# Nine passes of the sequence DFT as seven block products instead of eight, with two weight chunks prepared elsewhere

## The chip, the cores and the metric

The kernel runs on one core of a Trainium2 chip. The metric is the time of one execution in microseconds (us); the median of three runs stands for a kernel. Five engines run in order, each its own queue, and wait for one another by semaphores: TensorE (PE; PEld are its weight loads), VectorE (DVE), ScalarE (ACT), GpSimd (POOL) and SyncE (SP), which issues the transfers.

## The reference

One FNet block and one gated feed-forward, each behind a layer norm, on x of 2048 x 448:

```
a  = einsum("bsd,ed->bse", ln(x), dft_hid_re)
b  = einsum("bsd,ed->bse", ln(x), dft_hid_im)
h  = x + einsum("ts,bse->bte", dft_seq_re, a) - einsum("ts,bse->bte", dft_seq_im, b)
h2 = h + einsum("bsf,fd->bsd", gelu(ln(h) @ w_gate) * (ln(h) @ w_up), w_down)   # f = 1792
```

The DFT matrices are inputs, 2048 x 2048 and 448 x 448.

## The kernel before, in words

**Numbers in two halves.** Every float32 operand is split into a high and a low float16 half: `hi_part` (line 108, ScalarE) makes the high one, `lo_part` (lines 112 and 114, VectorE) the low one from the source and the high one. A product is then three matmuls, high by high, high by low, low by high.

**The sequence DFT** comes first: 64 steps (`N_STEPS`). Steps 0 to 15 accumulate rows 0 and 1 of the blocks; from step 16 on, four steps make a pass, that is half of one row pair `p`, from 2 to 7. A unit of weights, `ws`, belongs to each step: loaded by SP into `wr`, split by ScalarE and VectorE some steps ahead. A pass in the plain form is 4 x 24 matmuls `acc` of 128 x 448 (line 644). From step `FAST` = 32 on, a pass is done as seven block products (Strassen's scheme) instead of eight: 4 x 42 matmuls `acc_f` of 128 x 224 (line 521). For that, VectorE adds blocks of the unit (`fast_sums`, lines 471 to 473, tile `sums`), ScalarE and VectorE split the raw blocks and the sums (tiles `ws..._0` and `ws..._1`), and the combined operands T of the normed input, eight pairs of blocks, are made once by GpSimd (`t_sums`, tile `tx`) and split (`t_hi`, `t_lo`, tiles `t`). The accumulated banks are combined by `fast_out` (tile `e`) into `zs`.

**The hidden DFT** of each of the eight row pairs follows inside the sequence DFT. The rows are transposed (`z_turn`, line 669) and multiplied with `wh` in two groups, `y_p_0` and `y_p_1`: 21 matmuls of 448 columns each (line 730). Both groups of a pair use one bank of PSUM in turn. The residual is put into the bank first, by ScalarE (`hid_seed`, line 711), and the matmuls add to it; then ScalarE reads it three times (`hid_out`, lines 719 to 721). So the second group's matmuls wait for ScalarE's seed, which waits for its three reads of the first.

**Weights of the feed-forward** come in 14 chunks, `f`. `Weights` loads a chunk (`gu_raw`), makes sums (`gu_s`, lines 328 to 331, VectorE) and splits raw and sums (`gu_w`), and `store` writes it to memory for later units. Eight chunks are prepared beside the sequence DFT (`DFT_F`), the six others beside the feed-forward's units (`JIT_F`), where unit t uses chunk t at first. The feed-forward's first 14 units (lines 1044 and on) take 39 matmuls of 512 columns each; the hidden DFT of the last pair stands in the second of them.

**The order** is written out by hand. Two tables, `early` and `after`, say what is recorded ahead of a step's matmuls and what after its first or second half; each engine's queue has its instructions in the order in which they are recorded. The order within a step is: loads, split of plain units, `fast_sums` with its splits, `early`, matmuls with `after`:

```
    fast_at = [FAST + n for n in (-4, -2, -1)] + list(range(FAST + 1, N_STEPS - 2))
    ...
        if n in fast_at:
            unit = fast_at.index(n) + FAST
            fast_sums(unit)
            ...
            if n < FAST or n % 4 < 3:
                fast_raw(unit)
                fast_split(unit)
    ...
        at(early, m - 2, lambda p=p: hid_seed(p, 0))
        for g in range(2):
            place = last if g else (m, 0)
            at(after, place, lambda p=p, g=g: hid_mm(p, g), lambda p=p, g=g: hid_out(p, g))
            if g == 0:
                at(after, (m, 0), lambda p=p: hid_seed(p, 1))
```

For pair 1, `m` is 24 and `last` is (25, 0): `y_1_0` stands in the middle of step 24, `y_1_1` in the middle of step 25. For pair 2 they stand in steps 29 and 31.

**PSUM.** `ps_seq` gives its seven banks out in turn to `acc` and `acc_f`; when the DFT is over, `ps_ff` takes the same seven banks for the feed-forward, in the order of its names.

Of the kernel before, what the change touches and what calls it, by code (L numbers as in the profile page):

```python
# [32 lines left out]
def kernel(  # L33
# [39 lines left out]
    nc = tc.nc  # L73
# [31 lines left out]
    w_dram = [dram.tile([P, 28 * P], F16, name=f"w_dram{f}") for f in range(NF)]  # L105
# [65 lines left out]
    def w_tile(name, k):  # L171
        return ring.tile([P, 28 * P], F16, tag=f"w{k}", bufs=1, name=name)
# [126 lines left out]
    def ffn_transpose(q, j, parts):  # L299
        xs = ffn[q, j][2]  # L300
        ops = hops[q if q > 1 else 0]
        c = (2 * q + j if q < 2 else j) * P
        for n in parts:
            s0, s1 = ((0, 8), (8, 16), (16, 22), (22, 25))[n]
            nc.sync.dma_start_transpose(ops[:, s0:s1, c : c + P], xs[:, s0 * P : s1 * P])
# [110 lines left out]
    N_STEPS = NT + 8 * (NP - 2)  # L416
# [32 lines left out]

    FAST = N_STEPS - 32
    A_RAW = ("A12", "A11", "A22")
    FORMS = ("S3", "S1", "S2", "S4")
    T_OPS = ("T1", "T3", "T4", "T2")
# [289 lines left out]


    gu, gw = {}, {}
    DFT_F = ((13, 14, 0), (11, 16, 1), (9, 18, 0), (7, 20, 1), (5, 22, 0), (3, 24, 1), (1, 27, 0), (0, 30, 0))
    JIT_F = range(2, 13, 2)

    early, after = {}, {}

    def at(where, n, *what):
        where.setdefault(n, []).extend(what)
# [2 lines left out]
        at(early, 5 + 2 * n, lambda n=n: wh_load(n))  # L757
        at(early, 7 + 2 * n, lambda n=n: wh_split(n))

    def gw_first(f):  # L760
        gw[f] = w_tile(f"gw{f}", f)
        nc.sync.dma_start(gw[f], w_dram[f])

    for i, (f, n, k) in enumerate(DFT_F):
        ahead = 4 if i < 2 or n - DFT_F[i - 2][1] > 4 else 3
        at(after, (n - ahead, 0), lambda f=f, k=k: gu.update({f: Weights(f, k)}))
        at(early, n, lambda f=f: gu[f].sums())
        if f == 0:
            at(early, n + 2, lambda: gu[0].split(True))
            at(early, n + 3, lambda: gu[0].split(False), lambda: gw.update({0: gu[0].w}))  # L770
            at(after, (n + 5, 0), lambda: gu[0].store())
            continue
        at(early, n + 1, lambda f=f: gu[f].split(True))
        at(early, n + 2, lambda f=f: gu[f].split(False))
        at(after, (n + 3, 0), lambda f=f: gu[f].store())


    at(after, (N_STEPS - 3, 1), lambda: gw_first(1))

    turns = [(16, 0), (20, 1), (25, 1), (32, 0), (40, 0), (48, 0), (57, 0)]  # L780
    for p, (n, half) in enumerate(turns):
        b, j = divmod(p, 2)
# [14 lines left out]
        if b < 2:  # L797
# [4 lines left out]
            at(early, n2, lambda b=b, j=j: ffn_split(b, j))  # L802
            for k in range(4):
                at(after, (n2 + 1 + k // 2, k % 2), lambda b=b, j=j, k=k: ffn_transpose(b, j, (k,)))
    at(after, (N_STEPS - 5, 0), lambda: gu.update({JIT_F[1]: Weights(JIT_F[1], JIT_F[1] % 3)}))
    at(after, (N_STEPS - 6, 0), lambda: gu.update({JIT_F[0]: Weights(JIT_F[0], JIT_F[0] % 3)}))
    at(early, N_STEPS - 1, gelu_table)
    at(after, (N_STEPS - 2, 0), lambda: down_load(0), lambda: down_load(1))
    for j, n in ((6, 14), (7, 16), (0, 18), (1, 20), (4, 22), (5, 24), (2, 28), (3, 30)):
        at(early, n, lambda j=j: t_sums(j))  # L810
        at(after, (n, 1), lambda j=j: t_hi(j))
        at(after, (n + 1, 0), lambda j=j: t_lo(j))

# [470 lines left out]
    for q, t0, step, when in ((2, 5, 3, AT_A), (3, 14, 6, AT_B)):  # L1284
# [22 lines left out]
    right.close()  # L1307
    ps_ff = {
        tag: ctx.enter_context(tc.tile_pool(name=f"ps_{tag}", bufs=1, space=bass.MemoryType.PSUM, reuse_waits="tile"))
        for tag in ("a0", "a1", "a2", "a3", "Z", "Y", "X")  # L1310
    }
    ps_ff["tr"] = ps_tr

# [11 lines left out]
    for t in range(NF):  # L1325
        w = gu.get(t + 2) if t + 2 in JIT_F else None
        n = PREP_AT.get(t)
# [70 lines left out]
        do(t, 3)  # L1398
        if w:
            w.store()  # L1400
        if w and w.f + 4 in JIT_F:
            gu[w.f + 4] = Weights(w.f + 4, (w.f + 4) % 3)
        if n is not None and 2 <= n + 2 < NC:
            down_load(n + 2)
        do(t, 4)
# [10 lines left out]
    for t in range(NF, N_GU):  # L1416
# [169 lines left out]
```

## Time and profile before

| what | value |
|---|---|
| median of 3 runs (lowest, highest) | 699.07 us (698.65, 700.11) |
| the profiled execution | 699.87 us, of which its span 698.1 us |
| granted TensorE clock | 1.00 |
| busy shares: TensorE, VectorE, ScalarE, GpSimd | 99%, 82%, 56%, 24% |
| sequence DFT with seven hidden pairs | 6.2 to 336.9 us |
| steps 24 and 25 on TensorE | about 123.6 to 140.6 us |
| feed-forward | 336.9 to 698.1 us |

The span is from the first to the last instruction of the profiled execution; its time contains 1.8 us besides. In rows of a timeline the first number is the start from the span's beginning, the second the time taken, both in us; in brackets stands idle time ahead and what ended it. A row of groups ends with busy us, mean ns of one, and idle time ahead. Matmuls overlap, so a group's mean is longer than the distance from one to the next.

### The profile page before, as it was taken

What the parts mean: (1) busy time and instruction counts of PE and PEld (TensorE: products, weight loads), DVE (VectorE), ACT (ScalarE), POOL (GpSimd) and SP (SyncE); (2) the same over time, 40 slices, a digit from 0 to 9 for tenths busy, and PEclk for the clock granted to TensorE, in tenths of its full rate; (3) what the DMA queues carried; (4) which work ended last, traced back from release to release, by engine and by line L of the source; (5) the groups of instructions that cost most, each with busy time, mean ns of one, the idle gap of its engine ahead of it and who ended that gap; (6) DMA issues with size and microseconds to landing.
All of it is one profiled execution on the core that took longest, in us unless ns stands there. A gap on an engine that the chain in (4) does not pass through costs nothing.

```text
span 698.1 us, 13955 instructions
## 1 busy us (share of the span) xinstructions
PE 693.5 (99%) x5308; PEld 514.3 (74%) x5308; DVE 571.2 (82%) x1137; ACT 394.1 (56%) x781; POOL 166.6 (24%) x183
## 2 busy tenths in 40 slices
PE   9999999999999999999999999999999999999998
PEld 6555555555979888997644444469999999999997
DVE  6998996958999898995648797777778877899786
ACT  5876755746766555665427666555555453655631
POOL 0004754461202000000303333521120111232224
PEclk9999999999999999999999999999999999999999
DMA  8798679997968559384656877797869985887612
GB/s 272 243 244 271 143 260 268 249 251 286 194 197 189 163 125 237 127 196 178 158 187 239 286 235 247 202 325 237 234 206 334 243 300 176 313 283 273 226 50 80
DMA packets 113731, 155.81 MB, mean 223 GB/s; under 512 B 61696, under 2 KB 78208, under 8 KB 113664
## 3 DMA queue, kind: packets, MB, share of 16 engines
q1 hardware_dynamic: 113664, 154.92, 74.1%
q8 instruction: 41, 0.67, 0.4%
q14 instruction: 26, 0.21, 0.1%
HBM read 106.66 MB, written 34.34 MB: 202 GB/s over the span
## 4 chain that ended last, share of the span: by engine, by line
PE 96%; ACT 1%; DVE 1%; issue 1%; POOL 0%; ACTq 0%; POOLq 0%
PE acc L644 21%; PE acc_f L521 16%; PE acc_d L1248 15%; PE pY L1044 15%; PE pZ L1044 10%; PE pX L1044 10%; PE y L730 9%; PE pw L102 1%; ACT ws L108 1%; DVE ws L114 0%; ACT xn_h L243 0%; DVE sums L471 0%; ACT dn_w L108 0%; ACT v L974 0%; ACT y L721 0%
## 5 line engine op out<-in xcount | busy, mean ns | idle before, releaser
L1044 PEld LDWEIGHTS <-gw 128*128 128x128 f16 x1365 | 133.3, 98 | 42.7
L644 PE MATMUL acc<-xs,ws 128*128 128x448 f16 x768 | 146.9, 353 | 0.0
L521 PEld LDWEIGHTS <-ws 128*128 128x128 f16 x1344 | 128.7, 98 | 2.2 <-DVE ws L114 0.5
L644 PEld LDWEIGHTS <-ws 128*128 128x128 f16 x768 | 75.3, 98 | 70.3 <-issue 0.6
L1138 POOL TENSOR_TENSOR hs<-hs,c 128x256 f32<-128x256 f32 (+1 forms) x42 | 59.2, 1410 | 248.2 <-ACT c L1136 181.7
L1248 PE MATMUL acc_d<-wd,dn_w 128*128 128x224 f16 x1008 | 110.7, 259 | 0.0
L1248 PEld LDWEIGHTS <-dn_w 128*128 128x128 f16 x1008 | 96.9, 98 | 2.0
L521 PE MATMUL acc_f<-t,ws 128*128 128x224 f16 x768 | 92.2, 259 | 0.1
L1044 PE MATMUL pY<-hops,gw 128*128 128x256 f16 (+1 forms) x595 | 90.2, 294 | 0.0
L114 DVE SCALAR_TENSOR_TENSOR ws<-wr,ws 128x768 f16<-128x768 f32 (+2 forms) x66 | 73.8, 1119 | 10.4 <-ACT ws L108 10.1
L521 PE MATMUL acc_f<-xs,ws 128*128 128x224 f16 x576 | 73.5, 259 | 0.0
L108 ACT ACTIVATE ws<-wr 128x768 f16<-128x768 f32 (+2 forms) x66 | 60.4, 916 | 11.9 <-DMA wr<-in_w_seq_dram 11.0
L730 PE MATMUL y<-wh,z 128*128 128x448 f16 x336 | 66.2, 352 | 0.0
L1044 PE MATMUL pZ<-hops,gw 128*128 128x256 f16 (+1 forms) x385 | 61.7, 294 | 0.0
L1044 PE MATMUL pX<-hops,gw 128*128 128x256 f16 (+1 forms) x385 | 61.7, 294 | 0.0
L1089 ACT ACTIVATE pY<-pX 128x256 f32<-128x256 f32 (+1 forms) x42 | 18.4, 439 | 66.9 <-PE pX L1044 66.5
L730 PEld LDWEIGHTS <-z 128*128 128x128 f16 x336 | 32.9, 98 | 29.5 <-issue 0.3
L108 ACT ACTIVATE ws<-sums 128x512 f16<-128x512 f32 x64 | 39.0, 624 | 25.4 <-DVE sums L471 18.1
L1044 PEld LDWEIGHTS <-gu_w 128*128 128x128 f16 x273 | 26.6, 98 | 31.9
L1054 DVE SCALAR_TENSOR_TENSOR c<-pZ,u 128x256 f32<-128x256 f32 (+1 forms) x42 | 21.5, 511 | 34.7 <-PE pZ L1044 17.9
L1100 ACT ACTIVATE u<-pY 128x256 f32<-128x256 f32 (+1 forms) x42 | 19.1, 454 | 53.6 <-PE pY L1044 53.5
L112 DVE TENSOR_TENSOR dn_w<-dn_s,dn_w 128x640 f16<-128x640 f32 x48 | 42.2, 879 | 1.5 <-ACT dn_w L108 1.4
(148 smaller groups left out, 1005.1 us busy)
## 6 DMA issues: line engine op xcount, KB each, us to landing
gw<-w_dram SPq DMA_DIRECT2D x35, 896.0 KB, 6.6
wr<-in_w_seq_dram SPq DMA_DIRECT2D x100, 256.0 KB, 4.2
hid_dram<-hs SPq DMA_DIRECT2D x27, 512.0 KB, 5.9
hid<-hid_dram SPq DMA_DIRECT2D x54, 256.0 KB, 5.6
w_dram<-gu_w SPq DMA_DIRECT2D x14, 896.0 KB, 5.2
gu_raw<-in_w_gu_dram SPq DMA_DIRECT2D x28, 384.0 KB, 5.4
wr<-in_w_seq_dram SPq DMA_DIRECT2D x14, 512.0 KB, 5.7
x<-in_x_dram SPq DMA_DIRECT2D x16, 224.0 KB, 4.3
```

Source lines behind the costliest of these rows:

```text
L108: A.activation(dst, src, AF.Copy, scale=scale)
L112: V.tensor_sub(dst, src, hi)
L114: V.scalar_tensor_tensor(dst, src, scale, hi, op0=ALU.mult, op1=ALU.subtract)
L521: PE.matmul(fast_sum(n, k), fast_a(n, i, lw, a), fast_b(j, lx, b), start=j == 0 and m == 0 and k in (0, 1, 3, 5), stop=j == NT // 2 - 1 an ...
L644: PE.matmul(acc[key][:, :D], w[:, lw, block * P : (block + 1) * P], xs[c][:, lx, :], start=c == 0 and m == 0, stop=c == NT - 1 and m == 2,)
L730: PE.matmul(y[:, :D], z[p][:, lz, k, g * P : (g + 1) * P], wh[:, lw, k, :], start=p == NP - 1 and k == 0 and m == 0, stop=k == 6 and m == ...
L1044: PE.matmul(ps, w[:, wl, wa + ws, :], ops[:, m + ms, :], start=first and n == 0, stop=last and n == len(terms) - 1, skip_group_check=True,)
L1054: V.scalar_tensor_tensor(dst, ps, SC, other, op0=ALU.mult, op1=ALU.add)
L1089: A.activation(self.Y, self.X, AF.Copy)
L1100: A.activation(self.u2, self.Y, AF.Copy, scale=SC)
L1138: G.tensor_mul(c22, c22, self.cols(self.c12))
L1248: PE.matmul(ps, w[:, la, a, :], wd[n][:, lb, b, :], start=n == 0 and m == 0 and opens, stop=n == NC - 1 and m == 2, skip_group_check=True,)
```

## The change

The first step of the seven-product form moves from 32 to 28, so nine passes have it in place of eight. Chunk 3 leaves the sequence DFT and is prepared beside the feed-forward's second unit; chunk 1 leaves its middle and is prepared in steps 61 and 62, and unit 1 uses it from there instead of loading it back. Chunk 0 comes two steps earlier, and operands T of blocks 2 and 3 three steps earlier. The banks of the feed-forward get another order of names. The loads of `JIT_F`'s chunks are counted by one function.

```
-    FAST = N_STEPS - 32
+    FAST = N_STEPS - 36
...
-    DFT_F = ((13, 14, 0), (11, 16, 1), (9, 18, 0), (7, 20, 1), (5, 22, 0), (3, 24, 1), (1, 27, 0), (0, 30, 0))
-    JIT_F = range(2, 13, 2)
+    DFT_F = ((13, 14, 0), (11, 16, 1), (9, 18, 0), (7, 20, 1), (5, 22, 0), (0, 28, 0))
+    JIT_F = (1, 2, 3, 4, 6, 8, 10, 12)
+
+    def jit_load(i):
+        f = JIT_F[i]
+        gu[f] = Weights(f, f % 3)
...
-    def gw_first(f):
-        gw[f] = w_tile(f"gw{f}", f)
-        nc.sync.dma_start(gw[f], w_dram[f])
...
-            at(early, n + 2, lambda: gu[0].split(True))
-            at(early, n + 3, lambda: gu[0].split(False), lambda: gw.update({0: gu[0].w}))
-            at(after, (n + 5, 0), lambda: gu[0].store())
+            at(early, n + 1, lambda: gu[0].split(True))
+            at(early, n + 2, lambda: gu[0].split(False), lambda: gw.update({0: gu[0].w}))
+            at(after, (n + 4, 0), lambda: gu[0].store())
...
-    at(after, (N_STEPS - 3, 1), lambda: gw_first(1))
+    at(early, N_STEPS - 3, lambda: gu[1].sums())
+    at(early, N_STEPS - 2, lambda: gu[1].split(True))
+    at(early, N_STEPS - 2, lambda: gu[1].split(False), lambda: gw.update({1: gu[1].w}))
+    at(after, (N_STEPS - 1, 0), lambda: gu[1].store())
...
+    at(after, (N_STEPS - 6, 0), lambda: jit_load(0))
+    at(after, (N_STEPS - 5, 0), lambda: jit_load(1))
+    at(after, (N_STEPS - 1, 0), lambda: jit_load(2))
...
-    for j, n in ((6, 14), (7, 16), (0, 18), (1, 20), (4, 22), (5, 24), (2, 28), (3, 30)):
+    for j, n in ((6, 14), (7, 16), (0, 18), (1, 20), (4, 22), (5, 24), (2, 25), (3, 27)):
         at(early, n, lambda j=j: t_sums(j))
...
-        for tag in ("a0", "a1", "a2", "a3", "Z", "Y", "X")
+        for tag in ("a0", "a3", "Z", "Y", "X", "a1", "a2")
...
-        if w and w.f + 4 in JIT_F:
-            gu[w.f + 4] = Weights(w.f + 4, (w.f + 4) % 3)
+        if w and w.f < JIT_F[-2]:
+            jit_load(JIT_F.index(w.f) + 2)
```

What the program's queues hold at three places is shown next; the last number of a name counts tiles, the number ahead of it is the unit, chunk or pair. First, ScalarE in step 24 before: from the high half of unit 27 (`ws27`) over chunk 5 and the three reads of pair 1's first group to the seed of its second, `y_1_1`.

```order
L108 ACTIVATE ws27_1509<-wr27_1389 128x1024
L108 ACTIVATE gu_w5_1454<-gu_s5_1399 128x512 x2
L719 ACTIVATE hx0_1_1268,mv_h0_1_1564<-y_1_0_1411 128x448
L720 ACTIVATE mv_h0_1_1564<-mv_h0_1_1564 128x1
L721 ACTIVATE y_1_0_1411,mv_h0_1_1564<-y_1_0_1411,mv_h0_1_1564 128x448
L711 ACTIVATE y_1_1_1568<-hx0_1_1268 128x448
L108 ACTIVATE t45_1445<-tx5_0_1521 128x448
L108 ACTIVATE t45_1445<-tx5_1_1522 128x448
```

The seed follows the reads, and these follow chunk 5, with no sums of unit 28 among them. The same place after the change.

```order
L108 ACTIVATE ws27_1503<-wr27_1386 128x1024
L108 ACTIVATE ws28_0_1507<-wr28_1389 128x768
L108 ACTIVATE ws28_1_1508<-sums28_1506 128x512 x2
L108 ACTIVATE gu_w5_1454<-gu_s5_1399 128x512 x2
L719 ACTIVATE hx0_1_1268,mv_h0_1_1570<-y_1_0_1411 128x448
L720 ACTIVATE mv_h0_1_1570<-mv_h0_1_1570 128x1
L721 ACTIVATE y_1_0_1411,mv_h0_1_1570<-y_1_0_1411,mv_h0_1_1570 128x448
L711 ACTIVATE y_1_1_1574<-hx0_1_1268 128x448
L108 ACTIVATE t45_1445<-tx5_0_1524 128x448
L108 ACTIVATE t45_1445<-tx5_1_1525 128x448
```

Behind unit 27 the two rows of unit 28's raw blocks and sums are new, ahead of chunk 5, of the reads of `y_1_0` and of the seed `y_1_1`.

Second, VectorE at the same place before: from the low half of `zs2` and of T's block 4 (`t45` from `tx4`) on.

```order
L114 SCALAR_TENSOR_TENSOR zs2_1201<-acc2_10_1251,zs2_1201 128x448
L112 TENSOR_TENSOR t45_1445<-tx4_1413,t45_1445 128x448 x2
L114 SCALAR_TENSOR_TENSOR zs2_1201<-acc2_11_1252,zs2_1201 128x448
L114 SCALAR_TENSOR_TENSOR ws27_1509<-wr27_1389,ws27_1509 128x1024
L114 SCALAR_TENSOR_TENSOR gu_w5_1454<-gu_s5_1399,gu_w5_1454 128x512 x2
L328 TENSOR_TENSOR gu_s3_1516<-gu_raw3_1371 128x384
L329 TENSOR_TENSOR gu_s3_1516<-gu_s3_1516,gu_raw3_1371 128x384
L330 TENSOR_TENSOR gu_s3_1516<-gu_raw3_1371 128x256
L331 TENSOR_TENSOR gu_s3_1516<-gu_raw3_1371,gu_s3_1516 128x256
L114 SCALAR_TENSOR_TENSOR ws28_1588<-wr28_1448,ws28_1588 128x1024
```

Behind unit 27 chunk 5's last part and chunk 3's sums follow. And after the change.

```order
L114 SCALAR_TENSOR_TENSOR zs2_1201<-acc2_10_1251,zs2_1201 128x448
L112 TENSOR_TENSOR t45_1445<-tx4_1413,t45_1445 128x448 x2
L114 SCALAR_TENSOR_TENSOR zs2_1201<-acc2_11_1252,zs2_1201 128x448
L114 SCALAR_TENSOR_TENSOR ws27_1503<-wr27_1386,ws27_1503 128x1024
L471 TENSOR_TENSOR sums28_1506<-wr28_1389 128x512
L472 TENSOR_TENSOR sums28_1506<-sums28_1506,wr28_1389 128x256
L473 TENSOR_TENSOR sums28_1506<-wr28_1389,sums28_1506 128x256
L114 SCALAR_TENSOR_TENSOR ws28_0_1507<-wr28_1389,ws28_0_1507 128x768
L114 SCALAR_TENSOR_TENSOR ws28_1_1508<-sums28_1506,ws28_1_1508 128x1024
L114 SCALAR_TENSOR_TENSOR gu_w5_1454<-gu_s5_1399,gu_w5_1454 128x512 x2
L112 TENSOR_TENSOR t45_1445<-tx5_0_1524,t45_1445 128x448
L112 TENSOR_TENSOR t45_1445<-tx5_1_1525,t45_1445 128x448
```

The sums and low halves of unit 28 now stand behind the low half of unit 27, and those of chunk 3 are gone; up to unit 27 nothing differs.

Third, ScalarE at the end of the sequence DFT before: the reads of pair 6's second group, the roots for the norms, the table of gelu, the drain of the last group `e63` and the first copy of the feed-forward.

```order
L719 ACTIVATE hx3_0_3685,mv_h3_0_4001<-y_6_1_4005 128x448
L720 ACTIVATE mv_h3_0_4001<-mv_h3_0_4001 128x1
L721 ACTIVATE y_6_1_4005,mv_h3_0_4001<-y_6_1_4005,mv_h3_0_4001 128x448
L129 ACTIVATE sd_h2_1_4107<-mv_h2_1_3464,eps_t_85 128x2
L129 ACTIVATE sd_h3_0_4163<-mv_h3_0_4001,eps_t_85 128x2
L134 ACT_TABLE_LOAD
L134 ACTIVATE warm_90<-eps_t_85 128x1
L553 ACTIVATE e63_4179<-acc_f60_0_3943 128x224
L108 ACTIVATE zs7_3889<-e63_4179 128x2x448
```

The roots and the table follow the reads at once here. After the change chunk 1 (`gu_w1`) stands there too.

```order
L719 ACTIVATE hx3_0_3759,mv_h3_0_4075<-y_6_1_4079 128x448
L720 ACTIVATE mv_h3_0_4075<-mv_h3_0_4075 128x1
L721 ACTIVATE y_6_1_4079,mv_h3_0_4075<-y_6_1_4079,mv_h3_0_4075 128x448
L108 ACTIVATE gu_w1_4184<-gu_raw1_3926 128x512
L108 ACTIVATE gu_w1_4184<-gu_raw1_3926 128x256
L108 ACTIVATE gu_w1_4184<-gu_s1_4113 128x512 x2
L129 ACTIVATE sd_h2_1_4193<-mv_h2_1_3538,eps_t_85 128x2
L129 ACTIVATE sd_h3_0_4249<-mv_h3_0_4075,eps_t_85 128x2
L134 ACT_TABLE_LOAD
L134 ACTIVATE warm_90<-eps_t_85 128x1
L553 ACTIVATE e63_4265<-acc_f60_0_4017 128x224
L108 ACTIVATE zs7_3963<-e63_4265 128x2x448
```

The three rows of chunk 1 are new between the reads of `y_6_1` and the roots; all else keeps its order.

More of the change, by code (lines that the diff above doesn't have):

```diff
@@ L804 @@
                 at(after, (n2 + 1 + k // 2, k % 2), lambda b=b, j=j, k=k: ffn_transpose(b, j, (k,)))
-    at(after, (N_STEPS - 5, 0), lambda: gu.update({JIT_F[1]: Weights(JIT_F[1], JIT_F[1] % 3)}))
-    at(after, (N_STEPS - 6, 0), lambda: gu.update({JIT_F[0]: Weights(JIT_F[0], JIT_F[0] % 3)}))
+    at(after, (N_STEPS - 6, 0), lambda: jit_load(0))
+    at(after, (N_STEPS - 5, 0), lambda: jit_load(1))
+    at(after, (N_STEPS - 1, 0), lambda: jit_load(2))
     at(early, N_STEPS - 1, gelu_table)
     at(after, (N_STEPS - 2, 0), lambda: down_load(0), lambda: down_load(1))
-    for j, n in ((6, 14), (7, 16), (0, 18), (1, 20), (4, 22), (5, 24), (2, 28), (3, 30)):
+    for j, n in ((6, 14), (7, 16), (0, 18), (1, 20), (4, 22), (5, 24), (2, 25), (3, 27)):
         at(early, n, lambda j=j: t_sums(j))
```

## The prediction

> **What bounds the kernel now.** I read the page's busy shares first, then its chain of work that ended last, then TensorE's own waits.
>
> ```profile
> span 698.1 us, 13955 instructions
> PE 693.5 (99%) x5308; PEld 514.3 (74%) x5308; DVE 571.2 (82%) x1137; ACT 394.1 (56%) x781; POOL 166.6 (24%) x183
> PE 96%; ACT 1%; DVE 1%; issue 1%; POOL 0%; ACTq 0%; POOLq 0%
> ...
> PE pw L102 <- POOL sign_t L93: 1.4, 1, 1.4
> PE acc_d L1248 <- ACT v L974: 0.2, 1, 0.2
> ```
>
> TensorE is busy for 99% of the span and the chain runs through it for 96%. The last two rows are all of its waits: 1.6 us. So every microsecond of matmuls taken out counts in full, and so does every new wait of TensorE; there is no slack in it that could absorb one. The question is then whether the other engines still deliver in time, in the order that the change gives them. The chain in order of time has the prices (start, us, what):
>
> ```profile
> 1.35 4.87 PE pw L102 x44
> 6.22 89.00 PE acc L644 x468
> ...
> 125.87 3.97 PE y L730 x21
> 129.84 4.54 PE acc L644 x24
> 134.38 3.97 PE y L730 x21
> 138.35 18.16 PE acc L644 x96
> ...
> 278.73 16.10 PE acc_f L521 x168
> ```
>
> **The matmuls exchanged.** Steps 28 to 31, one pass, are 4 x 24 matmuls of 448 columns: 18.16 us (x96). As block products they are 4 x 42 of 224 columns: 16.10 us (x168). TensorE loses 2.06 us. Everything that it does besides stays, so without new waits the profiled execution's 699.87 us would become 697.8. That execution lies 0.8 us above the median of the three runs (699.07); I carry the sum over to the median.
>
> **What the earlier block products put in front of others.** Preparing a unit for block products needs VectorE's sums of blocks before ScalarE can make the high halves. Unit 28's preparation now stands in step 24 (its sequence load still stands two steps ahead). In ScalarE's queue it stands ahead of the drain of `y_1_0` and of the seed of `y_1_1`, and TensorE can't begin the second hidden product of pair 1 without that seed. Step 28, where the first such preparation stood, has no hidden product behind it; step 24 has two, at 125.87 and 134.38 above. ScalarE, then VectorE, then ScalarE and VectorE where the inserted work has a price (start, us, engine, line):
>
> ```profile
> 129.64 1.06 ACT L108 ACTIVATE ws<-wr 128x1024 f16<-128x1024 f32 x1
> 130.59 1.15 ACT L108 ACTIVATE gu_w<-gu_s 128x512 f16<-128x512 f32 x2
> 131.63 0.54 ACT L719 ACTIVATE hx<-y 128x448 f32<-128x448 f32 x1
> ...
> 133.28 0.55 ACT L711 ACTIVATE y<-hx 128x448 f32<-128x448 f32 x1
> 133.76 1.03 ACT L108 ACTIVATE t<-tx 128x448 f16<-128x448 f32 x2
> ...
> 134.88 1.21 DVE L114 SCALAR_TENSOR_TENSOR ws<-wr,ws 128x1024 f16<-128x1024 f32 x1
> 136.01 1.28 DVE L114 SCALAR_TENSOR_TENSOR gu_w<-gu_s,gu_w 128x512 f16<-128x512 f32 x2
> ...
> 155.87 1.37 DVE L114 SCALAR_TENSOR_TENSOR ws<-wr,ws 128x1024 f16<-128x1024 f32 x1 [1.85 <-ACT ws L108]
> 157.57 0.73 DVE L471 TENSOR_TENSOR sums<-wr 128x512 f32<-128x512 f32 x1 [0.33 <-DMA wr<-in_w_seq_dram]
> 157.57 0.84 ACT L108 ACTIVATE ws<-wr 128x768 f16<-128x768 f32 x1 [1.73 <-DMA wr<-in_w_seq_dram]
> 159.94 0.63 ACT L108 ACTIVATE ws<-sums 128x512 f16<-128x512 f32 x1 [0.97 <-DVE sums L473]
> 160.47 0.92 ACT L108 ACTIVATE gu_w<-gu_raw 128x512 f16<-128x512 f32 x2
> ...
> 183.28 0.67 DVE L471 TENSOR_TENSOR sums<-wr 128x512 f32<-128x512 f32 x1
> 184.90 0.63 ACT L108 ACTIVATE ws<-sums 128x512 f16<-128x512 f32 x1 [0.23 <-DVE sums L473]
> 185.44 1.14 ACT L108 ACTIVATE gu_w<-gu_s 128x512 f16<-128x512 f32 x2
> ```
>
> The seed ends at 133.28 + 0.55 = 133.83 and TensorE uses it at 134.38: a margin of 0.55 us. At that place VectorE is over 5 us behind ScalarE: the high half of unit 27 is made from 129.64, its low half from 134.88. Up to those two rows both queues are unchanged. The sums of unit 28 come right behind that low half, at 136.01 at the earliest, and ScalarE now has to wait for them.
>
> The new time of the seed: the sums begin at 136.01; ScalarE's second piece that reads them begins 1.62 us later where GpSimd stands still (183.28 to 184.90) and 2.37 us later where it works (157.57 to 159.94); the next instruction follows after 0.53 us (159.94 to 160.47); chunk 5's second high half takes 1.04 (130.59 to 131.63); the drain of `y_1_0` 1.65 (131.63 to 133.28); the seed 0.55. That is 141.4 with GpSimd still. But GpSimd now makes operand T of block 2 there, since its turn is moved from step 28 to 25 and its buffer comes free with the low half just ahead of 134.88; the two rows at 155.87 and 157.57, taken while GpSimd made the same operand, then hold. The low half costs 1.37 for 1.21, 0.16 more, and the seed ends at 136.01 + 0.16 + 2.37 + 0.53 + 1.04 + 1.65 + 0.55 = 142.3. TensorE stands from 134.38: 7.0 us at the low end, 7.9 at the high end. I take 7.9, by the rows with GpSimd at work. The lowest bound is a ScalarE that never waits for the sums: its own inserted work is 1.9 us (0.84 and twice 0.53), the seed at 135.7, the wait 1.4 us.
>
> Behind the seed on ScalarE stand the operands T and units 29 to 31, all needed by steps that come later by the same wait, so they lose nothing. Nor is anything else starved: VectorE gets the 7.9 us to catch up.
>
> **What a standing TensorE costs on top.** The trace has one start from rest, the kernel's own (count, min/median/max ns for the last row):
>
> ```profile
> L102 PEld LDWEIGHTS <-ident 128*128 128x128 f16 x44 | 4.6, 149 | 1.3 <-POOL sign_t L93 1.3
> ...
> L644 PEld LDWEIGHTS <-ws 128*128 128x128 f16 x768 | 75.3, 98 | 70.3 <-issue 0.6
> ...
> L644 PE MATMUL acc<-xs,ws x14: 352/353/581, 6.0 to 9.0; 128*128 128x448 f16 x14
> ```
>
> The 44 warm-up matmuls of 128 columns take 4.87 us. At the later 18.16 us for 96 x 448 columns (0.422 ns a column) they would take 2.38, so the start loses 2.5 us, and a weight load takes 149 ns for 98. The first real matmul still takes 581 ns for 353. So a start from rest costs 2.5 us, if 7.9 us of standing count as rest. The bounds are 0 and 2.5; I take 2.5, from the only start in the trace. The granted clock reads 1.00 in that stretch too, so that column will not show it; the weight loads' durations will.
>
> The Trainium skill, "TensorE: Matmul & The Clock Gate", Part 1 on the HAM clock gate, says that after an idle window of about 3.4 us the array falls to half its clock and gets it back after a busy window, the windows running freely. By that page the loss would be an estimated 1.7 to 3.4 us; the start in this trace agrees in kind, and no run here shows a stop in mid-kernel.
>
> **The other parts.** Chunk 3's preparation leaves steps 24 to 26 and chunk 1's steps 27 to 29; chunk 1 goes to steps 61 and 62, chunk 3 into the second unit. Chunk 0's comes two to three steps earlier, into the time that the wait gives: 0.
>
> ```profile
> 330.99 1.28 ACT L134 ACT_TABLE_LOAD   x1
> ...
> 333.52 0.36 ACT L553 ACTIVATE e<-acc_f 128x224 f32<-128x224 f32 x1 [1.03 <-PE acc_f L521]
> ...
> 338.49 0.58 ACT L1089 ACTIVATE pY<-pX 128x512 f32<-128x512 f32 x1
> ...
> 338.61 5.25 SPq L669 DMA_TRANSPOSE z<-zs  x4
> ...
> 339.55 1.29 PE pY L1044 x6
> ...
> L328 DVE TENSOR_TENSOR gu_s<-gu_raw 128x384 f32<-128x384 f32 x14 | 9.6, 684 | 0.2
> ...
> 344.30:363.28 18.98, 18.98 (x95) 9.11 (x93) 9.47 (x12) 5.72 (x10) 3.09 (x2) 1.00 0.68 223
> ```
>
> At the DFT's end chunk 1's high halves (0.92 and 1.15 us) come before the table load: the first drain `e` begins about 1.0 us late (330.99 + 2.07 + 1.48 = 334.5 for 333.5), which VectorE absorbs, since it waits for TensorE's last products anyway. The copy `pY` then keeps its margin of 339.55 - 339.07 = 0.48 us: cost 0, cover that wait. On SP the store of chunk 1 and the load of chunk 3 pass ahead of the last transposes at 338.61, and are issued by 335: 0. SP no longer loads prepared chunk 1 there. In the second unit (the window, in which PE, weight loads, DVE, ACT and POOL are the columns) VectorE works 9.47 of 18.98 us and ScalarE 5.72; chunk 3 adds to the one four sums of at most 0.68 us each, the row of `gu_s`, and low halves of at most twice 1.28 (136.01), 5.3 us in all, and 2.07 to the other: 0, covered by the two hidden products there. The banks in their new order: unit 0 gets three that the last group of products doesn't use, as before: 0. T operands of block 3 are made from step 27 and used in the second half of step 29: 0, two steps of cover turned into one.
>
> The sum: -2.06 + 7.9 + 2.5 = +8.3 us, so 699.07 + 8.3 = 707.4 us.
>
> **The rivals.** (a) The wait comes, but TensorE restarts at full rate: 699.07 - 2.06 + 7.9 = 704.9; 704.0 with GpSimd still. For it: 7.9 us may be too short a rest. (b) The other side, faster: the seed is in time, 699.07 - 2.06 = 697.0. It would need VectorE's last sum by 130.6 (134.38 - 0.53 - 1.04 - 1.65 - 0.55); against it stands VectorE's row at 134.88. (c) VectorE is level with ScalarE in most executions and only ScalarE's own 1.9 us count: 699.07 - 2.06 + 1.4 = 698.4, no change that can be told. (d) More waits follow, at the seed of `y_2_0` in step 29 or the restart takes twice as long: up to another 2.5 us and a wait of 1 us, 711. Against it: from the end of `y_1_1` to the start of `y_2_0` TensorE has two and a half of the old steps and one and a half of the new, some 17 us, and ScalarE some 8 us of work of its own.
>
> **How the numbers follow.** Wait with slow restart 0.62 (705.5 to 709.5), (a) 0.20, (b) 0.07, (c) 0.05, (d) 0.06. The range of 703.0 to 710.0 leaves out (b), (c), most of (d). Slower by over 0.2% (1.4 us, about what a measurement of this kernel can tell) is 0.62 + 0.20 + 0.06 = 0.88, the same 0.05, faster 0.07.
>
> **What would show it.** In the changed kernel's trace: TensorE waits for ScalarE's `y` for 7 to 8 us near 134 to 142, once; ScalarE waits for `sums` there; VectorE's `sums` begin at about 136; weight loads of about 150 ns and matmuls of some 580 ns in the 5 us behind the wait; 672 matmuls `acc` and 1512 `acc_f`, the group's 168 in 16.1 us; no wait at the first units. I am wrong if the seed ends before 134.4, if TensorE's idle time is under 4 us, or if it lies at the feed-forward's start.

## The result, and the profile after

| kernel | median, us (lowest, highest) | executions |
|---|---|---|
| before | 699.59 (698.65, 700.20) | 4 |
| after | 709.61 (708.99, 710.57) | 4 |

The changed kernel takes 1.0146 times as long (95% interval 1.0127 to 1.0165). Forecast were 707.4 us in a range of 703 to 710. The profiled execution of the changed kernel took 708.99 us, its span 707.2: 9.1 us more than the span of before.

The page's busy shares come first, then the chain by engine, then all waits of TensorE (us in total, how many, the longest).

```profile
span 707.2 us, 14130 instructions
PE 692.3 (98%) x5380; PEld 521.2 (74%) x5380; DVE 586.1 (83%) x1156; ACT 397.4 (56%) x789; POOL 171.8 (24%) x183
PE 89%; DVE 6%; issue 2%; ACT 2%; DMA 1%; POOL 0%; SPq 0%; DVEq 0%; ACTq 0%; POOLq 0%
PE y L730 <- ACT y L711: 9.2, 1, 9.2
PE pw L102 <- POOL sign_t L93: 1.4, 1, 1.4
PE acc_f L521 <- DVE ws L114: 1.1, 2, 0.7
PE acc_d L1252 <- ACT v L978: 0.2, 1, 0.2
```

TensorE's work shrank from 693.5 to 692.3 us, and the span grew all the same. The first row of waits is new: one wait of 9.2 us for ScalarE's `y`, at the place and of the kind that was forecast. The third row is new too, and was not foreseen. VectorE now stands in the chain for 6% of the span instead of 1%.

The place itself, as a timeline of TensorE, then ScalarE, then VectorE, then GpSimd (start, us, what; in brackets the idle time ahead and who ended it):

```profile
129.06 4.70 PE L644 MATMUL acc<-xs,ws 128*128 128x448 f16 x24
142.94 5.48 PE L730 MATMUL y<-wh,z 128*128 128x448 f16 x21 [9.18 <-ACT y L711]
...
137.53 0.63 ACT L108 ACTIVATE ws<-sums 128x512 f16<-128x512 f32 x1 [6.72 <-DVE sums L471]
139.13 0.63 ACT L108 ACTIVATE ws<-sums 128x512 f16<-128x512 f32 x1 [0.97 <-DVE sums L473]
142.34 0.55 ACT L711 ACTIVATE y<-hx 128x448 f32<-128x448 f32 x1
...
134.26 1.80 DVE L114 SCALAR_TENSOR_TENSOR ws<-wr,ws 128x1024 f16<-128x1024 f32 x1
135.99 1.51 DVE L471 TENSOR_TENSOR sums<-wr 128x512 f32<-128x512 f32 x1
137.54 0.76 DVE L472 TENSOR_TENSOR sums<-sums,wr 128x256 f32<-128x256 f32 x1
...
133.96 3.00 POOL L575 TENSOR_TENSOR tx<-xs 128x448 f32<-128x448 f16 x2 [4.32 <-DVE t L112]
```

Read it from the bottom up. GpSimd starts operand T of block 2 at 133.96. Beside it VectorE's low half of unit 27 takes 1.80 us and the first sum of unit 28 takes 1.51 us. ScalarE stands 6.72 us for that sum. The seed, at the end of its queue, starts at 142.34, and TensorE stands 9.18 us for the seed. Then its 21 matmuls take 5.48 us. For the first group of the same pair the same 21 take 4.14 us in this trace:

```profile
125.08 4.14 PE L730 MATMUL y<-wh,z 128*128 128x448 f16 x21
```

The windows around the wait show the clock (stretch, its length, busy us of PE, PEld, DVE, ACT and POOL with counts, granted clock, DMA share, GB/s):

```profile
132.00:136.00 4.00, 1.76 (x10) 0.78 (x8) 4.00 (x8) 0.00 (x0) 2.04 (x2) 1.00 1.08 238
136.00:140.00 4.00, 0.00 (x0) 0.00 (x0) 3.93 (x5) 1.50 (x3) 3.77 (x5) 0.86 0.92 214
140.00:144.00 4.00, 1.06 (x3) 0.40 (x3) 3.98 (x6) 3.75 (x10) 2.56 (x2) 0.50 0.00 1
144.00:148.00 4.00, 4.00 (x18) 1.91 (x17) 2.03 (x5) 0.00 (x0) 0.00 (x0) 0.79 1.15 265
148.00:152.00 4.00, 4.00 (x23) 2.05 (x21) 0.16 (x1) 3.42 (x9) 0.19 (x1) 1.00 0.77 149
```

The granted clock falls from 1.00 to 0.50 and comes back. If it has only these two values, 0.86 over 4 us means that it fell at 138.9, 5.1 us after the last matmul (129.06 + 4.70), and 0.79 that it returned at 145.7, 2.7 us after TensorE resumed. Those 2.7 us at half rate cost half of them, 1.4 us, and the matmuls' rows say the same: 5.48 - 4.14 = 1.34.

The third row of waits lies 120 us later, in the step of `y_4_1`. VectorE, SP and TensorE there:

```profile
242.26 0.69 DVE L471 TENSOR_TENSOR sums<-wr 128x512 f32<-128x512 f32 x1 [3.22 <-DMA wr<-in_w_seq_dram]
...
229.88 6.58 SPq L669 DMA_TRANSPOSE z<-zs  x4
236.50 1.26 SPq L305 DMA_TRANSPOSE hops<-xs  x1
237.86 8.25 SPq L432 DMA_DIRECT2D wr<-in_w_seq_dram  x8
...
261.03 0.56 PE L521 MATMUL acc_f<-xs,ws 128*128 128x224 f16 x4 [0.70 <-DVE ws L114]
262.16 0.84 PE L521 MATMUL acc_f<-t,ws 128*128 128x224 f16 x7 [0.39 <-DVE ws L114]
```

SP issues four transposes for 6.58 us and a fifth, then the loads of `wr`. VectorE stands 3.22 us for the first of them and is late from there on, until TensorE waits. The trace of before has a gap at the same place, of 2.61 us, but there VectorE's sums start at 233.23, 0.9 us ahead of `y_4_0` (234.09); here they start 0.35 us behind it (241.91). Why SP comes later against TensorE was not followed.

The account of the span, then: -2.06 for the exchanged pass (16.10 us for 168 matmuls, the rate of the undisturbed rows of block products in this trace), +9.18 for the wait, +1.34 for the slow matmuls behind it, +1.2 for the place near 250 us (from `y_4_0` to `y_4_1` it is 21.5 us, in the trace of before 20.3), -0.6 because `y_1_0` starts at 125.08 instead of 125.70. That is 9.1 of 9.1. The last term is not the change's: over the traces of this study the same instruction starts between 124.9 and 125.9.

### The profile page after: what moved, and what is told of

Its sections match the earlier page's. It is cut to its first block, busy times and chain, and to the rows that moved or that the text cites. A ratio compares the mean times of both kernels' runs of the same rounds, so it can differ in the third digit from the quotient of the medians.

```text
span 707.2 us, 14130 instructions
## 1 busy us (share of the span) xinstructions
PE 692.3 (98%) x5380; PEld 521.2 (74%) x5380; DVE 586.1 (83%) x1156; ACT 397.4 (56%) x789; POOL 171.8 (24%) x183
## 4 chain that ended last, share of the span: by engine, by line
PE 89%; DVE 6%; issue 2%; ACT 2%; DMA 1%; POOL 0%; SPq 0%; DVEq 0%; ACTq 0%; POOLq 0%
PE acc L644 17%; PE acc_d L1252 15%; PE acc_f L521 15%; PE pY L1048 15%; PE pX L1048 9%; PE pZ L1048 9%; PE y L730 8%; DVE ws L114 2%; DVE sums L471 1%; ACT ws L108 1%; PE pw L102 1%; DVE e L550 1%; DVE sums L472 1%; DMA wr<-in_w_seq_dram 1%; DVE xs L112 0%
## 5 line engine op out<-in xcount | busy, mean ns | idle before, releaser
L1048 PEld LDWEIGHTS <-gw 128*128 128x128 f16 x1287 | 125.8, 98 | 33.6
L521 PEld LDWEIGHTS <-ws 128*128 128x128 f16 x1512 | 144.7, 98 | 3.8 <-DVE ws L114 1.8
L644 PE MATMUL acc<-xs,ws 128*128 128x448 f16 x672 | 127.9, 352 | 0.0
L644 PEld LDWEIGHTS <-ws 128*128 128x128 f16 x672 | 65.7, 98 | 61.2
L521 PE MATMUL acc_f<-t,ws 128*128 128x224 f16 x864 | 103.8, 259 | 0.4 <-DVE ws L114 0.4
L521 PE MATMUL acc_f<-xs,ws 128*128 128x224 f16 x648 | 82.8, 259 | 0.7 <-DVE ws L114 0.7
L1048 PE MATMUL pY<-hops,gw 128*128 128x256 f16 (+1 forms) x561 | 81.9, 289 | 0.0
L1048 PEld LDWEIGHTS <-gu_w 128*128 128x128 f16 x351 | 34.2, 98 | 40.9
L1048 PE MATMUL pX<-hops,gw 128*128 128x256 f16 (+1 forms) x363 | 56.3, 289 | 0.0
L1048 PE MATMUL pZ<-hops,gw 128*128 128x256 f16 (+1 forms) x363 | 56.3, 289 | 0.0
L114 DVE SCALAR_TENSOR_TENSOR ws<-sums,ws 128x1024 f16<-128x1024 f32 x36 | 45.2, 1255 | 1.2 <-ACT ws L108 0.8
```

Of the source, the lines that this page charges most:

```text
L114: V.scalar_tensor_tensor(dst, src, scale, hi, op0=ALU.mult, op1=ALU.subtract)
L521: PE.matmul(fast_sum(n, k), fast_a(n, i, lw, a), fast_b(j, lx, b), start=j == 0 and m == 0 and k in (0, 1, 3, 5), stop=j == NT // 2 - 1 an ...
L644: PE.matmul(acc[key][:, :D], w[:, lw, block * P : (block + 1) * P], xs[c][:, lx, :], start=c == 0 and m == 0, stop=c == NT - 1 and m == 2,)
L1048: PE.matmul(ps, w[:, wl, wa + ws, :], ops[:, m + ms, :], start=first and n == 0, stop=last and n == len(terms) - 1, skip_group_check=True,)
```

## The experiments

All medians stand against that of the kernel before from the same set of runs: 699.05 for the first four kernels, 699.09 for the next four, 699.15 and 698.90 for the two pairs at the end.

**1. Unit 28's preparation one step later.** It then stands behind the seed on ScalarE. Nothing else is changed.

```
-    fast_at = [FAST + n for n in (-4, -2, -1)] + list(range(FAST + 1, N_STEPS - 2))
+    fast_at = [FAST + n for n in (-3, -2, -1)] + list(range(FAST + 1, N_STEPS - 2))
```

> The changed kernel with one number other: unit 28's preparation for block products stands in step 25 instead of 24, behind the seed of y_1_1 on ScalarE and on VectorE. Theory (the loss is TensorE's wait for that seed, 9.2 us, and the slow restart behind it, 1.5 us): the wait is gone, y_1_1 takes 3.97 us, and what is left is -2.06 us for the ninth pass and about 1 us of waits near step 48: 698 to 699 us, against 699.6 before. Rival (the loss lies in the block products of the ninth pass or in the moved chunks, and the wait only hides other waits behind it): new waits of several us in steps 28 to 36, 703 us or more.

Measured: 699.37 us, ratio 1.0003 (0.9994 to 1.0012). TensorE's waits that differ from those of before, and the two hidden products:

```profile
PE acc_f L521 <- DVE t L112: 1.0, 1, 1.0
PE acc_f L521 <- DVE ws L114: 0.6, 2, 0.4
...
133.55 4.14 PE L730 MATMUL y<-wh,z 128*128 128x448 f16 x21
...
160.69 0.93 PE L521 MATMUL acc_f<-t,ws 128*128 128x224 f16 x8 [0.98 <-DVE t L112]
```

The 9.2 us are gone, and with them the slow matmuls: `y_1_1` starts right behind the step's first half and takes 4.14 us. So one number in `fast_at` carries the loss of 10 us. But the kernel should now be 2 us faster than before, and it isn't. In the profiled execution two places with short new waits have taken most of that: operand T of block 3, late in step 29 (0.98 us), and a unit late near 250 us (from `y_4_0` to `y_4_1` 21.0 us for 20.3 before).

**2. GpSimd out of the way.** Operand T of block 2 one step later, with the preparation of unit 28 left where the change put it.

```
-    for j, n in ((6, 14), (7, 16), (0, 18), (1, 20), (4, 22), (5, 24), (2, 25), (3, 27)):
+    for j, n in ((6, 14), (7, 16), (0, 18), (1, 20), (4, 22), (5, 24), (2, 26), (3, 27)):
```

> The changed kernel with operand T of block 2 made from step 26 instead of 25, so that GpSimd stands still while VectorE makes the sums of unit 28. Theory (GpSimd at work made VectorE's low half of unit 27 and its sums slower, about 2.0 us of the 9.2 us wait): the sums start earlier and take 1.5 us, the wait is about 7.2 us, the time about 707.4 us. Rival (GpSimd has no part in it): the wait stays 9.2 us and the time 709.6 us.

Measured: 712.82 us, ratio 1.0189 (1.0168 to 1.0210). TensorE, then VectorE:

```profile
141.05 5.65 PE L730 MATMUL y<-wh,z 128*128 128x448 f16 x21 [7.08 <-ACT y L711]
165.86 0.93 PE L521 MATMUL acc_f<-t,ws 128*128 128x224 f16 x8 [3.12 <-DVE t L112]
...
134.47 1.21 DVE L114 SCALAR_TENSOR_TENSOR ws<-wr,ws 128x1024 f16<-128x1024 f32 x1
135.61 0.68 DVE L471 TENSOR_TENSOR sums<-wr 128x512 f32<-128x512 f32 x1
```

With GpSimd still, the same two rows of VectorE take 1.21 and 0.68 us instead of 1.80 and 1.51, and the wait is 7.08 instead of 9.18 us. This is the low end that the prediction gave (7.0). So GpSimd's work beside VectorE is 2.1 us of the wait. The total missed: operand T of block 3 follows T of block 2 on GpSimd, comes later in turn, and TensorE waits 3.12 us for it. That accounts for the profiled execution, which took 709.75 us, 0.8 more than that of the changed kernel. The other three took 712.15 to 713.75, and no trace shows what held them longer.

**3. The rest of the change alone.** The plain first step of before (32) and the old order of the banks, with all moves of chunks and of T kept.

```
-    FAST = N_STEPS - 36
+    FAST = N_STEPS - 32
...
-        for tag in ("a0", "a3", "Z", "Y", "X", "a1", "a2")
+        for tag in ("a0", "a1", "a2", "a3", "Z", "Y", "X")
```

> The rest of the change alone: eight passes as block products as before (first step 32) and the old order of banks, but with chunks 0, 1 and 3 and operands T of blocks 2 and 3 moved as in the change. Theory (these parts cost nothing): 699.6 us within 0.7, no wait of TensorE over 0.5 us. Rival (the chunks at the DFT's end and in the second unit have a price): 701 us or more, with waits at the feed-forward's start.

Measured: 699.29 us, ratio 0.9998 (0.9989 to 1.0007). TensorE has the two waits of before and no other. The moves cost nothing and bring nothing by themselves, to within 0.8 us.

**4. and 5. TensorE kept busy during the wait.** Matmuls of 64 columns, whose result nothing reads, ahead of `y_1_1`; first 120, then 300.

```
+        if (p, g) == (1, 1):
+            for _ in range(300):
+                PE.matmul(acc[3, 0, 0][:, D:], wh[:, 0, 0, 0:P], wh[:, 0, 0, 0 : 512 - D], start=False, stop=False, skip_group_check=True)
```

> The changed kernel with 120 additional matmuls of 64 columns on TensorE ahead of y_1_1's first, into columns of a bank that nobody reads, so that TensorE works for about 7 of the 9.2 us instead of standing still. Theory (the restart's loss comes from standing still): the seed comes at the same time, y_1_1 takes 3.97 us instead of 5.48, the granted clock stays 1.00, and the time falls by 1.5 us to about 708.1 us. Rival (the slow matmuls behind the wait have another cause): y_1_1 still takes 5.5 us, 709.6 us.

> The changed kernel with 300 small matmuls of 64 columns, whose result nothing reads, in TensorE's queue ahead of y_1_1, so that it does not rest while it waits for the seed (the 120 of the run before took only 3.7 of the 9.2 us). Theory (a stop costs its length, and about 1.5 us besides for the slower matmuls behind it): the wait row of y_1_1 falls to under 1 us, its 21 matmuls take 3.97 to 4.15 us instead of 5.48, the granted clock stays at 1.00 from 132 to 152 us, and the time falls by 1.3 to 1.5 us, to 708.1 to 708.4. Rival (the slower matmuls come from something else at that place, such as the operands' arrival): y_1_1 still takes 5.5 us, 709.6. If 300 outlast the wait, the time rises by what they outlast it.

Measured: 709.67 us with 120 (ratio 1.0151, 1.0137 to 1.0165), 707.38 us with 300 (1.0119, 1.0105 to 1.0132). First the row of the 120 and that of `y_1_1` behind them, then the rows with 300 and two of their windows.

```profile
133.73 3.66 PE L730 MATMUL acc<-wh 128*128 128x64 f16 x120
143.08 5.56 PE L733 MATMUL y<-wh,z 128*128 128x448 f16 x21 [5.68 <-ACT y L711]
```

```profile
133.60 4.36 PE L730 MATMUL acc<-wh 128*128 128x64 f16 x144
138.93 4.98 PE L730 MATMUL acc<-wh 128*128 128x64 f16 x156 [0.96 <-issue]
143.75 4.14 PE L733 MATMUL y<-wh,z 128*128 128x448 f16 x21
...
140.00:144.00 4.00, 3.89 (x127) 3.71 (x124) 3.99 (x6) 3.78 (x10) 2.60 (x2) 1.00 0.12 42
144.00:148.00 4.00, 4.00 (x23) 2.08 (x22) 2.05 (x5) 0.02 (x1) 0.00 (x0) 1.00 1.11 266
```

The 120 were too few: one takes 30 ns (3.66 / 120), so 5.68 us of rest were left, and `y_1_1` was still slow. That run doesn't answer the question, but it shows that a rest of 5.7 us costs as much as one of 9.2. With 300 there is no rest longer than 0.96 us, the clock stays at 1.00, and `y_1_1` takes 4.14 us: the slow matmuls come from the rest, not from anything else at that place. The rival on this point is out. The 300 outlast the seed (it ends at 142.91, the matmuls start at 143.75) by 0.8 us. So the fall of the time is no measure of the restart. Between the two profiled executions it is 1.7 us: 0.8 lost by the later start of `y_1_1`, 1.3 gained by its matmuls, and 1.1 gained near 250 us, where this trace has no wait (20.4 us from `y_4_0` to `y_4_1`). Why it has none was not followed.

**6. to 8. Where the ninth pass's gain went.** These three keep experiment 1's place for unit 28 and add one move each. In 6 the preparation of pair 3's rows (`tt` on VectorE, splits, transposes) goes to later steps. In 7 chunk 0 and pair 1's sums also go behind T of block 3. In 8 GpSimd also makes T of block 3 a step earlier, and pair 1's norm comes a step later.

```
-            n0, n1, n2 = ((21, 22, 23), (27, 28, 32), (36, 37, 38), (44, 45, 46))[p]
+            n0, n1, n2 = ((21, 22, 23), (27, 28, 32), (36, 37, 38), (49, 50, 51))[p]
```

In 7, besides:

```
-    DFT_F = ((13, 14, 0), (11, 16, 1), (9, 18, 0), (7, 20, 1), (5, 22, 0), (0, 28, 0))
+    DFT_F = ((13, 14, 0), (11, 16, 1), (9, 18, 0), (7, 20, 1), (5, 22, 0), (0, 29, 0))
...
-            n0, n1, n2 = ((21, 22, 23), (27, 28, 32), (36, 37, 38), (49, 50, 51))[p]
+            n0, n1, n2 = ((21, 22, 23), (27, 30, 32), (36, 37, 38), (49, 50, 51))[p]
```

In 8, on top of 7:

```
-        at(early, m1 + p // 3 if p < 5 else N_STEPS - 7 + p, lambda b=b, j=j: ffn_rstd(b, j))
+        at(early, m1 + (p == 1) + p // 3 if p < 5 else N_STEPS - 7 + p, lambda b=b, j=j: ffn_rstd(b, j))
...
-            n0, n1, n2 = ((21, 22, 23), (27, 30, 32), (36, 37, 38), (49, 50, 51))[p]
+            n0, n1, n2 = ((21, 22, 23), (28, 30, 32), (36, 37, 38), (49, 50, 51))[p]
...
-    for j, n in ((6, 14), (7, 16), (0, 18), (1, 20), (4, 22), (5, 24), (2, 25), (3, 27)):
+    for j, n in ((6, 14), (7, 16), (0, 18), (1, 20), (4, 22), (5, 24), (2, 25), (3, 26)):
```

> Unit 28's preparation in step 25 as in the first experiment, and the feed-forward's preparation of pair 3's rows (VectorE's tt, its splits and the transposes) in steps 49 to 51 instead of 44 to 46. Theory (the ninth pass's 2.06 us were lost in that experiment to two places where VectorE is late, 1.0 us in step 29 and 0.9 us near step 48): the second loss goes, 699.4 - 0.9 = 698.5 us, and TensorE's row of acc_f behind ws of VectorE near 250 us goes. Rival (the lateness near step 48 is the load of wr, not VectorE's work): no change, 699.4.

> As the run before it in this set, and chunk 0's preparation one step later (29 for 28) and the sums of pair 1's rows two steps later (30 for 28), so that nothing of either stands in VectorE's queue ahead of operand T of block 3. Theory (those 4.9 us of VectorE's work, from 154.58 to 159.48, make T late): the low half of T ends at about 159.7 instead of 160.6, the wait of 1.0 us in step 29 falls to 0.1, 697.5 us, and with it the ninth pass gains what it was costed at, to within 0.5 us of 697.0. Rival (GpSimd, which ends at 158.56, sets T): the wait falls by less than half, 698.2 or more.

> As the run before it in this set, and GpSimd makes operand T of block 3 in step 26 instead of 27, ahead of the reciprocal roots of pair 1 and of what follows them (the norm of pair 1 in step 28 instead of 27). Theory: GpSimd starts T when its buffer comes free, at about 144.5 instead of 150.6, T is ready by 155 and no wait is left in step 29: 697.0 to 697.4 us. Rival (GpSimd now works beside VectorE's sums of units 29 to 31 and slows them, from 0.68 to about 1.1 us for the first row of each, and these come late): a wait for ws or sums in steps 29 to 31 takes the place of it, 698 us or more.

Measured: 701.97 us (ratio 1.0045, 1.0029 to 1.0061), 703.78 us (1.0064, 1.0051 to 1.0077), 702.57 us (1.0049, 1.0037 to 1.0061). All three are slower than experiment 1, where 1 to 2.4 us of gain were expected. Of 6, TensorE's longest new wait, VectorE's wait, and SP ahead of it; then of 7, the late units.

```profile
282.00 0.84 PE L521 MATMUL acc_f<-t,ws 128*128 128x224 f16 x7 [1.34 <-DVE ws L114]
...
274.76 0.69 DVE L471 TENSOR_TENSOR sums<-wr 128x512 f32<-128x512 f32 x1 [6.62 <-DMA wr<-in_w_seq_dram]
...
263.49 7.07 SPq L669 DMA_TRANSPOSE z<-zs  x4
```

```profile
PE acc_f L521 <- DVE ws L114: 3.8, 7, 0.9
...
178.78 0.84 PE L521 MATMUL acc_f<-t,ws 128*128 128x224 f16 x7 [0.60 <-DVE ws L114]
188.37 1.13 PE L521 MATMUL acc_f<-xs,ws 128*128 128x224 f16 x10 [0.91 <-DVE ws L114]
```

The wait aimed at is gone each time (in 6 near 250 us, in 7 and 8 in step 29), and new ones for VectorE's `ws` stand further on, 3.0, 3.8 and 3.6 us in all. In 6 SP's next group of transposes takes 7.07 us from 263.49, VectorE stands 6.62 us for a load that SP issues behind it (1.91 us at that place in experiment 1), and TensorE waits up to 1.34 us for the unit. In 7 units from 178 to 188 us are late, behind the work put off, and others near 282 to 287 us. So none of these moves found room. The rows suggest that what is put off makes something else late, on VectorE or behind SP; no run separates the two.

**9. to 12. The smallest moves.** Back to experiment 1. VectorE's short rows `tt` of pairs 1 and 3 are moved, and in 11 and 12 the norm of pair 3 ahead of them (`xn_h`, ScalarE) as well. No transpose moves.

```
-            n0, n1, n2 = ((21, 22, 23), (27, 28, 32), (36, 37, 38), (44, 45, 46))[p]
+            n0, n1, n2 = ((21, 22, 23), (27, 29, 32), (36, 37, 38), (44, 45, 46))[p]
```

That is 10. In 9, 11 and 12 the last triple, pair 3's, is (44, 46, 46), (43, 44, 46) and (41, 42, 46) instead: the step of the norm, of `tt`, and of the split.

> Unit 28's preparation in step 25 as in the first experiment (699.4), and nothing else than VectorE's short rows of L254 to L263 (tt, 1.6 us together) moved one step back at two places: for pair 1 from step 28 to 29, behind operand T of block 3, and for pair 3 from step 45 to 46, behind the sums of the unit there. No transpose moves, so nothing that SP issues. Theory (in the first experiment VectorE's queue, not a load, sets both late places): T's low half ends at about 159.8 instead of 160.65, so the wait in step 29 falls from 1.0 to 0.1 us, and the low half of the unit near 250 us comes 1.6 us earlier, so both short waits there go: 699.4 - 0.9 - 0.9 = 697.6 us, faster than before by about the ninth pass's 2 us less what is lost elsewhere. Rival (VectorE is full over the whole stretch from 134 to 190 us, so that each thing moved back makes the next one late, as the runs with 1 to 3 us of new waits suggest): 699 us or more, with a wait for ws in steps 30 to 36.

> The same with pair 1's rows alone moved from step 28 to 29; pair 3's stay. Theory: the wait in step 29 goes, the loss of 0.9 us near 250 us stays, 698.5 us. Rival: a wait for ws in steps 30 to 36 takes its place, 699.4 or more.

> The run with pair 1's rows moved (698.7), and pair 3's norm and VectorE's rows of L254 to L263 (tt) one step earlier, in steps 43 and 44 for 44 and 45; splits and transposes stay. Theory (VectorE is late near 250 us because it stood still before: 0.91 us for ScalarE's ws behind the norm, xn_h): the norm then no longer stands ahead of that ws, the idle 0.91 us go, and TensorE's row of 0.4 us near 251 us and the unseen 0.4 beside it with them: 697.9 us. Rival (VectorE is late anyway, since the load of wr held it 2.4 us at 231 us): no change, 698.7.

> The same rows three steps earlier instead, norm in step 41 and tt in step 42, so that on VectorE they stand ahead of the sums that wait for wr at about 229 to 231 us, where VectorE stands still for 2.4 us. Theory (the work fits into VectorE's gap at SP's transposes): the 1.6 us are hidden there, no wait near 250 us is left, 697.8 us. Rival (no change): 698.7. A third case: ScalarE waits in step 41 for the roots that GpSimd makes, and a wait for ws appears there, 699 us or more.

| experiment | median, us | ratio, 95% interval |
|---|---|---|
| 9: pair 1 later, pair 3 later | 699.13 | 0.9999 (0.9991 to 1.0008) |
| 10: pair 1 later | 698.66 | 0.9992 (0.9983 to 1.0001) |
| 11: pair 1 later, pair 3 a step earlier | 697.38 | 0.9976 (0.9965 to 0.9986) |
| 12: pair 1 later, pair 3 three steps earlier | 697.20 | 0.9973 (0.9964 to 0.9982) |

Number 10 does what was expected of it: the wait for T falls from 0.98 to 0.17 us. Number 9 loses that again, with a wait of 0.79 us for a unit at 259.65: its time is the rival's, though not its place (steps 30 to 36). Putting pair 3's rows off doesn't help. Bringing them forward does. VectorE of 10, of 11 and of 12 from 229 us on:

```profile
231.11 0.69 DVE L471 TENSOR_TENSOR sums<-wr 128x512 f32<-128x512 f32 x1 [2.37 <-DMA wr<-in_w_seq_dram]
243.70 0.96 DVE L114 SCALAR_TENSOR_TENSOR ws<-wr,ws 128x768 f16<-128x768 f32 x1 [0.91 <-ACT ws L108]
245.88 0.42 DVE L254 TENSOR_TENSOR tt<-xn_h 128x256 f32<-128x256 f32 x1
```

```profile
232.01 0.69 DVE L471 TENSOR_TENSOR sums<-wr 128x512 f32<-128x512 f32 x1 [2.67 <-DMA wr<-in_w_seq_dram]
242.09 0.42 DVE L254 TENSOR_TENSOR tt<-xn_h 128x256 f32<-128x256 f32 x1
```

```profile
229.76 0.42 DVE L254 TENSOR_TENSOR tt<-xn_h 128x256 f32<-128x256 f32 x1
231.44 0.69 DVE L471 TENSOR_TENSOR sums<-wr 128x512 f32<-128x512 f32 x1
```

In 10 VectorE stands 2.37 us for SP's load and 0.91 for ScalarE's `ws`, and then has `tt` to do when it is late. In 12 `tt` stands in the first of these gaps (229.76 to 231.3), the sums start at 231.44, only 0.3 us later than in 10, and no wait is left near 250 us: from `y_4_0` to `y_4_1` it is 20.07 us, which is the 16.10 + 3.97 of the work alone. But 11 has the same 20.07 us and no wait there either, and in it the first gap stays idle (2.67 us). There the norm and `tt` come one step earlier, and the second gap, the 0.91 us for ScalarE's `ws`, is gone, as was expected of that run. So what helps is that the norm and `tt` come earlier, ahead of the units that were late; filling the first gap is one way to it and not the only one. The kernel of 12 is 1.9 us faster than before by its ratio (0.0027 x 699; 1.3 to 2.5), which contains the 2.06 us that the exchanged matmuls were costed at. It has the lowest median of this study, but 11 can't be told from it.

## Why the prediction was right

The mechanism and its place were as forecast. The total was 2.2 us low, 0.5 of it because the kernel before, too, stood higher in this set of runs (699.59 for 699.07). The sizes of the wait and of the restart were off by 1.3 and 1.2 us in opposite directions, and it is luck that these two nearly cancel.

- **The matmuls exchanged, -2.06.** Right: 16.10 us for a pass. Experiments 11 and 12 show it as a gain of the whole kernel, once the preparation keeps up.
- **The wait, +7.9.** It was 9.18: mis-sized by 1.3. The queue order was read rightly, and without GpSimd the sum was right to 0.1 us (7.08 in experiment 2 for 7.0). The step that failed is the price of VectorE beside GpSimd, taken as 1.37 for the low half and 2.37 for the sums. The prediction says that GpSimd made the same operand at the place of those rows. It didn't: there it was at operand T of block 3, and beside VectorE's two rows ran its later instructions, of 224 columns. Here its first two additions, of 448 columns, ran beside the low half and into the first sum. The low half took 1.80, and the second piece of ScalarE that reads the sums began 139.13 - 135.99 = 3.14 us after them. Which instructions of GpSimd slow VectorE by how much was not tested, but the trace of before has a low half that was nearly as slow beside GpSimd, one step ahead of the place in question:

```profile
127.95 1.68 DVE L114 SCALAR_TENSOR_TENSOR ws<-wr,ws 128x1024 f16<-128x1024 f32 x1
```

- **The restart, +2.5.** It was 1.34, inside its bounds of 0 and 2.5. The kernel's own start was no good measure of a stop within it: there the loss lasts 4.87 us of matmuls, here 2.7.
- **"That column will not show it."** Wrong. The granted clock fell to 0.50. From a column that reads 1.00 at the kernel's start it did not follow that it can't show a stop. What was named in its place, weight loads of about 150 ns and matmuls of some 580, is there too, but for 2.7 us and not for 5 (count, min/median/max ns; 98 and 352 are the usual ones). The counts forecast, 672 `acc` and 1512 `acc_f`, are there.

```profile
L730 PEld LDWEIGHTS <-z x6: 147/147/147, 143.3 to 145.1; 128*128 128x128 f16 x6
L730 PE MATMUL y<-wh,z x7: 530/577/577, 142.9 to 145.1; 128*128 128x448 f16 x7
```

- **The rule on the clock gate.** The Trainium skill, "TensorE: Matmul & The Clock Gate", Part 1 on the HAM clock gate, was right in kind: half clock after an idle window of about 3.4 us, back after a busy one. The falls here come 5.1 us after the last matmul in the changed kernel, 5.2 in experiment 4 and 3.4 in experiment 2 (from 0.82 and 0.67 as the granted clock of the 4 us window), and the return 2.7 to 3.1 us after the restart. The loss of 1.3 to 1.5 us lies below the 1.7 to 3.4 that the prediction estimated by that page of the Trainium skill.
- **"The other parts", 0.** Right as a whole by experiment 3, and the first units wait for nothing. That operand T of block 3 came in time was luck: without TensorE's 9 us of standing it is 0.98 us late (experiment 1). And one thing was missed: VectorE has more to do (586.1 us for 571.2) and few gaps, and its gap behind SP's transposes near 230 us, which cost 0.2 us before, now ends in a wait of TensorE: +1.2 in the profiled execution. Nothing in the sum looked at the block products behind the wait; "nor is anything else starved" was the step that failed, and experiments 11 and 12 show that an earlier norm and `tt` mend it.
- **The rivals.** (a), a restart at full rate: the clock refutes it. (b) and (c): refuted by the 9.18. (d): neither of its two parts came, for `y_2_0` waits for nothing and the restart was shorter; more waits did follow, but near 250 us.

What is not settled: the changed kernel's other executions took up to 1.6 us longer than the profiled one, and no trace shows where.

## What to carry to other kernels

When work is moved earlier, look up which engine its first instruction waits for, and how far that engine is behind the one in whose queue it is put: here 5 us, and everything queued behind it paid them. TensorE pays a rest twice, since after 3.4 to 5.2 us of rest its clock halved here and needed about 3 us of work to return. And where the helper engine has few gaps, work put off came back as the next wait, while 1.6 us of work brought forward, ahead of the place that was late, was free.

## What the runs showed of the hardware

- GpSimd beside VectorE is dear for instructions of VectorE that read two operands: the sum of 512 columns took 0.68 us alone and 1.51 beside it, the low half of 1024 columns 1.21 and 1.80. The Trainium skill, "SBUF — State Buffer", section on the two separate sides, says that an instruction of VectorE with two inputs in SBUF and one of GpSimd that reads SBUF take one pair of ports in turn, for a whole instruction each; the trace agrees in that both lengthen at once: GpSimd's first two additions took 3.00 us here, and 2.02 in experiment 2 where VectorE had nothing to do (its row follows).

```profile
153.34 2.02 POOL L575 TENSOR_TENSOR tx<-xs 128x448 f32<-128x448 f16 x2
```

- A rest of 5.7 us cost TensorE 1.42 us (5.56 for 4.14), one of 7.1 us 1.51, one of 9.2 us 1.34: between these lengths a longer rest costs no more.
- A matmul of 64 columns with its own weight load, of the same weights each time, took about 30 ns in a row of 120, half of what I had put it at.
